# A sparse-attention and MLP kernel: another order and named PSUM banks for batch 0, and batch 1's steps moved by a group

## The chip, the cores and the metric

The kernel runs on one core of a Trainium2 chip. A core has a matrix engine (TensorE, PE in the profile), VectorE (DVE), ScalarE (ACT), GpSimd (POOL) and SyncE (SP), which work side by side and wait for each other through semaphores. Matmuls write to PSUM, a memory of 8 banks of 128 partitions x 512 fp32; VectorE and ScalarE read it from there. DMA queues move data between HBM and on-chip SBUF; SyncE and GpSimd issue them here. The metric is the device time of the program in microseconds, lower is better.

## The reference

Eight batches of eight heads, 576 tokens each, head size 64. Heads 0 to 3 attend locally (a token sees itself and the 31 before it), heads 4 to 7 with a stride (a token sees the earlier tokens whose position is equal modulo 32). The result goes through an MLP with a squared ReLU.

```python
scores = scale * np.matmul(q, k.transpose(0, 1, 3, 2))
mask_local = (rel >= 0) & (rel < stride)                                  # heads 0-3
mask_strided = (rel >= 0) & (pos[None, :] % stride == pos[:, None] % stride)  # heads 4-7
attn = softmax(np.where(masks, scores, -1e9))
x = np.matmul(attn, v).transpose(0, 2, 1, 3).reshape(4608, 512)
out = np.square(np.maximum(x @ w_in, 0)) @ w_out      # 512 -> 2048 -> 512
```

Inputs and output are float32; the kernel computes in bf16 with fp32 accumulation.

## The kernel before

**Units and chunks.** Heads go in pairs: unit u = 4*batch + pair. Pairs 0 and 1 are local, 2 and 3 strided; so units 0 and 1 are batch 0's local pairs, 2 and 3 its strided ones. Each pair's attention output is a 128-row strip of `xt[pair]`, which holds x transposed, all 4608 tokens. The MLP runs in 9 chunks of 512 tokens. A chunk has 16 groups of `mm1` (four matmuls over the four `xt` strips, L662, then ReLU on ScalarE, L668, and the square on VectorE, L669) and 16 groups of `mm2` (four matmuls each, L684; after every fourth a copy, L688, and a store).

**Order by hand.** The scheduler is off: every engine runs its instructions in the order in which the program issues them. The start (L814 to L850) issues the first loads, constants and masks. Then `BATCH0` is a list of steps that make batch 0's attention, ending with the first three `mm1` groups, split by `xt` strip (`P0 P23 P1`, strips 0, then 2 and 3, then 1; `FIRST` is that order). Then come the numbered groups of the MLP, and `PLAN` says which attention steps of later batches are issued ahead of which group. Groups 0 to 2 are empty (they are the `P` steps), 3 to 15 are the rest of chunk 0's `mm1`, 16 to 31 its `mm2`, 32 onward chunk 1, which needs batch 1.

**Steps** (unit or batch in the name, then the engine: a = ScalarE, v = VectorE, g = GpSimd):
- `c0q`: cast of q of local unit 0 to bf16 (L298). `T0q`: six TensorE transposes (L453) and a copy from PSUM (L460).
- `W0q0`, `W0q1`: the same for the strided heads of batch 0, in two tiles (L332, L337).
- `S0`: scores of unit 0 in two halves, each with two rows (heads): in batch 0 a matmul adds the mask as a bias (L482), then the scores (L493) and an exp per row and half (L503).
- `N2`: strided row sums by a matmul with ones (L583), reciprocal as Ln (L585) and Exp(-x) (L586). `O2`: strided values times weights (L607) and the multiply by the reciprocal into `xt` (L609).
- `D0.0`, `D0.1`: local values in two parts (L622), reciprocal (L627), multiply (L628). `E0`: transposes (L644) and the copy into `xt` (L647).
- `w2`: two matmuls on zeros into bank `py` (L719). `m`: memsets of zero blocks (L812). `H`: a shifted copy of v (L411).
- For batch 1: `l` loads q or k of the local pairs, `r` the strided rows, `U` and `V` the values, `o` a quarter of w_out (L429), `B` and `k` spread strided v and k (L398, L366), `s1.0` to `s1.2` strided scores (L538), `x1.0` to `x1.2` their sums, reciprocals and multiplies into `xt` (L549 to L568).

**PSUM.** Eight banks, each a tile of its own: two `ph`, one `py`, five `pt`. `bank("pt")` hands out the next in turn; in batch 0 the turn goes over the five `pt` and the two `ph`. A step that gets a bank waits until its last reader is done.

**Queues.** `load_qk_hw(0)` loads unit 0's q and k in fp32 through SyncE's queue; everything else until L850 goes through GpSimd's: strided q and k of batch 0, unit 1's q and k (L291), values, and w_in.

Of the kernel before, what the change touches and what calls it, by code (L numbers as in the profile page):

```python
# [12 lines left out]

FIRST = (0, 2, 3, 1)
NP = 3
BATCH0 = """
    c0qv c0ka T0qa c1kg w2 T0kv w2 S0 mk1v c1qv W0k0a w3 W0q0v W0k1a W0q1v T1qv w2 T1kv S2 S1 H0v D0.0 D0.1 S3
    D1.0 N3 D1.1 N2 E0a O3 O2 E1a w1 P0 P23 P1  # L20
"""
PLAN = """
0: l1q4+5 l1k4+5 z
1: r1q U1 mv1g
3: o0
4: r1k V1 mk0v
5: o1 l2k8+9 mbg
6: o2 o3 V2 mv0v
7: c4qv
8: c5qv  # L30
9: c4kv
10: l2q8+9 c5ka T4qa
11: T4kv T5qa
12: W1q0v T5ka
13: S4
14: W1q1v
16: W1k0a S5! B10v
17: W1k1a
18: D4.0 k10v mrg C2q C2k
19: k11v  # L40
20: D4.1 s1.0 B11v
21: D5.0 s1.1 U2
22: l3k12+13 s1.2
23: D5.1
24: E5v x1.0
26: X2k l3q12+13
27: E4v x1.1 c9kv
28: V3
29: x1.2 c8qv
30: c8ka c9qv  # L50
31: X2q
34: C3q B20v
35: T8kv B21v
37: T9kv
# [109 lines left out]
def kernel(  # L164
# [44 lines left out]
    banks = {nm: [psum.tile([128, 512], FP32, name=f"{nm}{i}") for i in range(n)]  # L209
             for nm, n in (("ph", 2), ("py", 1), ("pt", 5))}  # L210

    banks["b0"] = banks["pt"] + banks["ph"]
    in_b0 = [True]

    def bank(nm):
        if in_b0[0] and nm == "pt":
            nm = "b0"
        t = banks[nm].pop(0)
        banks[nm].append(t)
        while id(t) in unread:  # L220
            run_due(lambda x: x[1] == unread[id(t)])
        return t

    unread = {}

# [240 lines left out]
    def step_S(u, mode=0):  # L466
# [7 lines left out]
        s["e"] = e  # L474
        pss = [[None, None], [None, None]]
        for half in range(2):
            for row in range(2):
                pss[row][half] = bank("pt")
                if u < 4:
                    bias = bias_l[:, half].rearrange("p t c -> p (t c)") if local \  # L480
                        else bias_s.rearrange("p t c -> p (t c)")
                    nc.tensor.matmul(pss[row][half][0:kn, 0:S // 2], ident[0:kn, 0:kn], bias,  # L482
                                     start=True, stop=False, skip_group_check=True)
            for i in range(hn):
                t = half * hn + i
                klo = w * t
                for row in range(2):
                    rows = slice(64 * row, 64 * row + 64)
                    if not local:
                        lhsT, rhs = (a[rows, t // 4, t % 4, :] for a in (kT, qT))  # L490
                    else:
                        lhsT, rhs = kT[rows, klo:klo + kn], qT[rows, w * t:w * (t + 1)]
                    nc.tensor.matmul(pss[row][half][0:kn, w * i:w * (i + 1)], lhsT, rhs,  # L493
                                     start=u > 3, stop=True, skip_group_check=u < 4)

        for row in range(2):
            for half in range(2):
# [13 lines left out]
        if u < 4:  # L511
            for half in range(2):
                for row in range(2):
                    expo(row, half)
            return
        if mode == 1:
            for row in range(2):
                for half in range(2):
# [57 lines left out]
    def step_N(u):  # L576
        e, hw = st[u]["e"], S // 2
        kn = 128 if is_local(u) else SP_
        for half in range(2):
            pn = bank("pt")  # L580
# [4 lines left out]
            nc.scalar.activation(rv0[:, u, hw * half:hw * (half + 1)], pn[:, 0:hw], AF.Ln)  # L585
        nc.scalar.activation(rv0[:, u], rv0[:, u], AF.Exp, scale=-1.0)  # L586

    def step_O(u):
        s = st.pop(u)
        e, hw = s["e"], S // 2  # L590
        for half in range(2):
            po = bank("pt")
            rv = rv0[:, u, hw * half:hw * (half + 1)]
            if is_local(u):
                for t in range(NL // 2):
                    for h in range(2):
                        c = S * h + hw * half + QL * t
                        nc.tensor.matmul(po[64 * h:64 * h + 64, QL * t:QL * (t + 1)],
                                         vls[u][:, h, NL // 2 * half + t, 0:D], e[:, c:c + QL],
                                         start=True, stop=True)  # L600
                nc.vector.tensor_tensor(xt[u][:, hw * half:hw * (half + 1)], po[:, 0:hw], rv, op=ALU.mult)
                continue
            w = SP_
# [5 lines left out]
            nc.vector.tensor_tensor(  # L609
                xt[u][:, 0:S].rearrange("c (p j r) -> c p j r", j=NJ // 2, r=2)[:, :, :, half],  # L610
                po[:, 0:hw].rearrange("c (j p) -> c p j", p=SP_),
                rv.rearrange("c (j p) -> c p j", p=SP_), op=ALU.mult)
# [108 lines left out]
    idle = xt[0][:, T - 512:T]  # L721

    def first_part(kks):
        in_b0[0] = False
        for ff in range(NP):
            mm1(0, ff, kks, FIRST, None if ff < 2 else "py")

    def run_step(word):
        op, arg = word[0], word[1:]
        if op == "w":  # L730
            warm(int(arg))
# [72 lines left out]
    def memset_later(which, eng):  # L804
# [5 lines left out]
        else:  # L810
            t = (kbds if which[0] == "k" else vbds)[int(which[1])]
            eng.memset(t.rearrange("p n c -> p (n c)").bitcast(FP32), 0.0)  # L812
# [112 lines left out]
```

## Time and profile before

| | us |
|---|---|
| three timed runs | 304.89, 305.20, 307.47 |
| median | 305.2 |
| the profiled execution, in all | 304.5 |
| its span, first to last instruction | 302.8 |
| from the span's start to the first MLP matmul (L662) | 19.9 |
| matmuls of all 9 chunks, L662 and L684 on the chain that ended last | 38% and 37% of the span |

The profile is of one execution. TensorE's granted clock was 1.00 throughout. DMA engines are 97% busy in the first 10 us of the span and near that or above in the next 70. A timeline row gives the start, the duration, the engine, the line, what is written from what, the shapes, the number of instructions merged into the row, and in brackets the idle time of that engine before it and what ended it. A row of the list of waits says which engine and line waited for which, the total, how often, and the longest.

### The profile page before, as it was taken

How to read it: one execution, taken by the hardware profiler on the slowest of the kernel's cores; microseconds unless marked ns; L12 is line 12 of the kernel's file. 1: busy time of each engine (PE TensorE's matmuls, PEld its weight loads, DVE VectorE, ACT ScalarE, POOL GpSimd, SP SyncE). 2: the span in 40 equal slices, each digit the busy share in tenths (PEclk: the TensorE clock that was granted, in tenths of full speed). 3: DMA queues.
4: the chain of work that ended last, by engine and by line, in shares of the span. 5: the costliest groups of instructions: out<-in, count | busy, mean ns of one | idle time of the engine just before them, and what ended most of it. 6: DMA issues, size and time to landing. Idle time of an engine off the chain costs nothing.

```text
span 302.8 us, 5715 instructions
## 1 busy us (share of the span) xinstructions
PE 292.9 (97%) x2143; PEld 146.3 (48%) x2181; DVE 179.5 (59%) x465; ACT 173.2 (57%) x342; POOL 71.3 (24%) x105
## 2 busy tenths in 40 slices
PE   8988999999999999999999999999999999999996
PEld 3543555445555544454454445444454444444444
DVE  5668686888578686585558494676486524104400
ACT  3677853777657744773387446744775447216611
POOL 8734834007213018064300830000000000000000
PEclk9999999999999999999999999999999999999999
DMA  7999999997999999999998999511110110010011
GB/s 149 189 207 196 188 201 187 143 206 124 149 183 159 143 183 151 150 161 119 184 173 153 141 190 153 118 38 67 54 23 19 73 69 0 35 71 35 0 71 70
DMA packets 93643, 37.28 MB, mean 123 GB/s; under 512 B 78956, under 2 KB 87750, under 8 KB 93616
## 3 DMA queue, kind: packets, MB, share of 16 engines
q0 software_dynamic: 54960, 18.82, 62.8%
q1 hardware_dynamic: 38512, 18.03, 30.5%
q8 instruction: 17, 0.28, 0.4%
q14 instruction: 10, 0.08, 0.1%
q10 hardware_dynamic: 144, 0.07, 0.1%
HBM read 38.21 MB, written 9.44 MB: 157 GB/s over the span
## 4 chain that ended last, share of the span: by engine, by line
PE 89%; DVE 3%; issue 2%; DMA 2%; ACT 2%; POOL 0%; DVEq 0%; ACTq 0%; POOLq 0%
PE ph L662 38%; PE ph L684 37%; PE pt L493 2%; DMA w_out_b<-in_k_dram 2%; PE pt L622 2%; PE pt L538 1%; PE pt L552 1%; PE ph L709 1%; PE pt L453 1%; PE pt L549 1%; PE py L684 1%; DVE g_sb L669 1%; DVE xt L562 1%; PE pt L684 1%; ACT r L668 1%
## 5 line engine op out<-in xcount | busy, mean ns | idle before, releaser
L662 PE MATMUL ph<-xt,w_in_b 128*128 128x512 bf16 x548 | 130.5, 379 | 2.3 <-ACT xt L647 1.0
L684 PE MATMUL ph<-w_out_b,g_sb 128*128 128x512 bf16 x513 | 119.7, 379 | 0.8
L668 ACT ACTIVATE r<-ph 128x512 bf16<-128x512 f32 x142 | 84.8, 599 | 35.3 <-PE ph L662 30.2
L669 DVE TENSOR_TENSOR g_sb<-r 128x512 bf16<-128x512 bf16 x144 | 60.4, 422 | 63.8 <-ACT r L668 63.0
L662 PEld LDWEIGHTS <-w_in_b 128*128 128x128 bf16 x576 | 53.0, 97 | 59.7 <-issue 2.3
L684 PEld LDWEIGHTS <-g_sb 128*128 128x128 bf16 x560 | 51.7, 97 | 57.4 <-DVE g_sb L669 0.5
L688 ACT COPY y<-ph 128x512 f32<-128x512 f32 x33 | 19.4, 589 | 53.0 <-PE ph L684 53.0
L562 DVE TENSOR_TENSOR xt<-pt,rv 64x144 bf16<-64x144 f32 x84 | 34.0, 404 | 18.4 <-ACT rv L555 17.3
L503 ACT ACTIVATE e<-pt 128x288 bf16<-128x288 f32 (+1 forms) x68 | 24.0, 417 | 7.7 <-PE pt L493 7.7
L554 ACT ACTIVATE rv<-pt 128x432 f32<-128x432 f32 (+1 forms) x21 | 10.5, 501 | 13.8 <-PE pt L549 13.8
L628 DVE TENSOR_TENSOR x_l<-pt,rinv 96x384 bf16<-96x384 f32 x30 | 16.6, 554 | 1.0
L568 DVE TENSOR_TENSOR xt<-pt,rv 64x270 bf16<-64x270 f32 (+1 forms) x28 | 10.9, 432 | 8.5 <-ACT rv L555 8.4
L509 DVE TENSOR_TENSOR e<-e,mask_all 128x576 bf16<-128x576 bf16 x28 | 12.4, 453 | 3.9 <-ACT e L503 3.6
L539 ACT ACTIVATE e<-pt 128x432 bf16<-128x432 f32 (+1 forms) x21 | 10.4, 497 | 6.6 <-PE pt L538 6.6
L350 POOL DMA_DIRECT2D q_t<-in_q_dram x6 | 3.6, 602 | 44.0 <-DMA qT_s<-q_t 44.0
L419 POOL DMA_DIRECT2D vl<-in_v_dram x7 | 10.1, 1437 | 12.2 <-PE ph L684 6.9
L279 POOL DMA_DIRECT2D k_l<-in_k_dram x16 | 11.9, 751 | 2.9 <-PE pt L552 2.9
L279 POOL DMA_DIRECT2D q_l<-in_q_dram x16 | 11.8, 740 | 2.8 <-DMA k_l<-in_k_dram 1.4
L622 PEld LDWEIGHTS <-e 128*128 128x128 bf16 x192 | 9.1, 97 | 5.8 <-issue 0.4
L555 ACT ACTIVATE rv<-rv 128x432 f32<-128x432 f32 (+1 forms) x21 | 11.2, 533 | 0.7
L622 PE MATMUL pt<-vl,e 128*128 128x65 bf16 x180 | 9.9, 193 | 0.0
L350 POOL DMA_DIRECT2D k_t<-in_k_dram x6 | 3.2, 538 | 25.2 <-DMA kT_s<-k_t 25.2
(130 smaller groups left out, 216.8 us busy)
## 6 DMA issues: line engine op xcount, KB each, us to landing
out_dram<-y SPq DMA_DIRECT2D x35, 256.0 KB, 3.9
vl<-in_v_dram POOLq DMA_DIRECT2D x7, 384.0 KB, 12.4
w_in_b<-in_moe_w_in_dram POOLq DMA_DIRECT2D x4, 512.0 KB, 13.1
w_out_b<-in_moe_w_out_dram POOLq DMA_DIRECT2D x4, 512.0 KB, 13.1
q_t<-in_q_dram POOLq DMA_DIRECT2D x7, 288.0 KB, 6.6
k_t<-in_k_dram POOLq DMA_DIRECT2D x7, 288.0 KB, 5.8
v_st<-in_v_dram POOLq DMA_DIRECT2D x7, 216.0 KB, 8.5
k_l<-in_k_dram POOLq DMA_DIRECT2D x16, 72.0 KB, 7.9
```

The lines of the kernel that those rows point to most:

```text
L279: nc.gpsimd.dma_start(out=t[:, :, hh, :], in_=src[b, 2 * p + hh].rearrange("(t p) d -> p t d", p=QL))
L503: nc.scalar.activation(e[0:kn, lo:lo + S // 2], pss[row][half][0:kn, 0:S // 2], AF.Exp, scale=scale)
L509: nc.vector.tensor_tensor(x, x, m, op=ALU.mult)
L555: nc.scalar.activation(rv, rv, AF.Exp, scale=-1.0)
L562: nc.vector.tensor_tensor(to[:, :, NJ * part:NJ * (part + 1), par], of, by, op=ALU.mult)
L622: nc.tensor.matmul(po[:, n, :], e[:, c:c + 128], rhs[:, NL * part + n, 0:D + 1], start=True, stop=True)
L628: nc.vector.tensor_tensor(x, po[0:QL, :, 0:D], rinv[0:QL].to_broadcast([QL, NL, D]), op=ALU.mult)
L662: nc.tensor.matmul(ph, w_in_b[:, kk, 128 * ff:128 * (ff + 1)], xt[kk][:, 512 * c:512 * (c + 1)], start=(kk == order[0]), stop=(kk == order ...
L668: nc.scalar.activation(r, ph, AF.Relu)
L669: later(1, lambda: nc.vector.tensor_tensor(g[:, ff, :], r, r, op=ALU.mult))
L684: nc.tensor.matmul(py, g[:, ff, 128 * j:128 * (j + 1)], w_out_b[:, ff, :], start=(ff == 0), stop=(ff == 15))
L688: nc.scalar.copy(y, py)
```

## The change

The batch-0 list is reordered: unit 1's casts, transposes and scores come directly behind unit 0's and ahead of the strided transposes and scores; the casts and copies are dealt out to other engines; the MLP's first part runs over strips 2, then 0, then 1 and 3. Unit 1's q and k come through SyncE's queue in fp32, as unit 0's do, instead of GpSimd's.

All eight banks are now one tile `psb`. In batch 0 each step names its banks after a slash, and where it works on two banks, the number is the first of two neighbours: `S2/0,2` puts the first half into banks 0 and 1, the second into 2 and 3; `S0/0,1` puts the first into 0 and 1, the second into 1 and 2. The exps of a half, the Ln of `N`, the multiply of `O` and the reciprocal and multiply of `D` (new function `step_D0`, both parts at once) are one instruction over two banks.

In the plan, most steps of batch 1 move to the next group; the first quarter of w_out is loaded ahead of strided q; the memset of one block goes from VectorE in batch 0 to GpSimd; the E copies of batch 1 go to ScalarE; x1.1 and x1.2 come a group earlier.

```diff
-FIRST = (0, 2, 3, 1)
+FIRST = (2, 0, 1, 3)
 BATCH0 = """
-    c0qv c0ka T0qa c1kg w2 T0kv w2 S0 mk1v c1qv W0k0a w3 W0q0v W0k1a W0q1v T1qv w2 T1kv S2 S1 H0v D0.0 D0.1 S3
-    D1.0 N3 D1.1 N2 E0a O3 O2 E1a w1 P0 P23 P1
+    c0qa c0kv T0qa/6 w1/7 T0kv/4 w1/7 S0/0,1 c1qv c1kv T1qv/5 T1ka/6 w2/7 S1/0,1 W0q0v/4 W0q1v/5 w3/7 W0k0a/4
+    W0k1v/5 w1/7 S2/0,2 H0v S3/4,0 D0/2 N2/6 D1/4 E0a/0 O2/2 N3/6 O3/4 E1a/1 w2/5 P2 P0 P13
 """
 PLAN = """
 0: l1q4+5 l1k4+5 z
-1: r1q U1 mv1g
-3: o0
-4: r1k V1 mk0v
-5: o1 l2k8+9 mbg
-6: o2 o3 V2 mv0v
-7: c4qv
-8: c5qv
-9: c4kv
-10: l2q8+9 c5ka T4qa
-11: T4kv T5qa
-12: W1q0v T5ka
-13: S4
-14: W1q1v
-16: W1k0a S5! B10v
-17: W1k1a
-18: D4.0 k10v mrg C2q C2k
-19: k11v
-20: D4.1 s1.0 B11v
-21: D5.0 s1.1 U2
-22: l3k12+13 s1.2
-23: D5.1
-24: E5v x1.0
-26: X2k l3q12+13
-27: E4v x1.1 c9kv
-28: V3
-29: x1.2 c8qv
-30: c8ka c9qv
-31: X2q
+1: o0 mv1g
+3: r1q mk0v
+4: r1k mk1g
+5: U1 V1 mbg mv0v
+6: o1 o2
+7: o3 l2k8+9 V2
+8: c4qv
+9: c5qv
+10: c4kv
+11: l2q8+9 c5ka T4qa
+12: T4kv T5qa
+13: T5ka
+14: W1q0v
+15: S4 W1q1v
+17: W1k0a S5! B10v
+18: W1k1a
+19: k10v mrg C2q C2k D4.0
+20: k11v D4.1
+21: s1.0 B11v D5.0
+22: s1.1 U2
+23: l3k12+13 s1.2 D5.1
+24: x1.0
+25: E4a
+26: x1.1 X2k l3q12+13
+27: E5a
+28: x1.2 V3
+29: c9kv
+30: c8qv
+31: c8ka c9qv X2q
...
+    psb = psum.tile([128, 8, 512], FP32, name="psb")
+    all_banks = [psb[:, i] for i in range(8)]
+    banks = {"ph": [all_banks[i] for i in (6, 2)], "py": [all_banks[7]],
+             "pt": [all_banks[i] for i in (3, 1, 0, 4, 5)]}
+    places = []
     def bank(nm):
-        if in_b0[0] and nm == "pt":
-            nm = "b0"
+        if places:
+            return all_banks[places.pop(0)]
...
+    def bank_pair():
+        i = places.pop(0)
+        return all_banks[i:i + 2], psb[:, i:i + 2]
...
         for half in range(2):
+            if u < 4:
+                (pss[0][half], pss[1][half]), both = bank_pair()
...
+            if u < 4:
+                hw = S // 2
+                nc.scalar.activation(e[0:kn, 0:2 * S].rearrange("p (r c) -> p r c", r=2)[:, :, hw * half:hw * (half + 1)],
+                                     both[0:kn, :, 0:hw], AF.Exp, scale=scale)
...
+    def step_D0(u):
...
+        pos, both = bank_pair()
+        for part, po in enumerate(pos):
+            for n in range(NL):
+                c = QL * (NL * part + n)
+                nc.tensor.matmul(po[:, (D + 1) * n:(D + 1) * (n + 1)], e[:, c:c + 128], rhs[:, NL * part + n, 0:D + 1],
+                                 start=True, stop=True)
...
+        nc.vector.reciprocal(r, po[:, :, :, D:D + 1])
+        nc.vector.tensor_tensor(s["x"].rearrange("p (t h) d -> p h t d", h=2), po[:, :, :, 0:D],
+                                r.to_broadcast([QL, 2, NL, D]), op=ALU.mult)
...
     load_qk_hw(0)
+    load_qk_hw(1)
     load_str_rows(0, "q")
...
-    load_qk_local_sw(0, (1,))
     load_v0()
```

More of the change, by code (lines that the diff above doesn't have):

```diff
@@ L208 @@
     psum = ctx.enter_context(tc.tile_pool(name="psum", bufs=1, space=PS))
[L209 to L213, printed above, removed]
+    psb = psum.tile([128, 8, 512], FP32, name="psb")
[3 more added lines that the diff above has]
+    places = []
     def bank(nm):
-        if in_b0[0] and nm == "pt":
-            nm = "b0"
+        if places:
+            return all_banks[places.pop(0)]
         t = banks[nm].pop(0)
@@ L269, in load_qk_hw @@
             c = n_s + 8 * S if name == "q" else n_s
+            c += 24 * D * (u if name == "k" else -u)
             t = b0[0:QL, c:c + 24 * D].bitcast(FP32).rearrange("p (h c) -> p h c", h=2)
@@ L476, in step_S @@
         for half in range(2):
+            if u < 4:
+                (pss[0][half], pss[1][half]), both = bank_pair()
             for row in range(2):
-                pss[row][half] = bank("pt")
+                if u > 3:
+                    pss[row][half] = bank("pt")
                 if u < 4:
@@ L494, in step_S @@
                                      start=u > 3, stop=True, skip_group_check=u < 4)
+            if u < 4:
+                hw = S // 2
+                nc.scalar.activation(e[0:kn, 0:2 * S].rearrange("p (r c) -> p r c", r=2)[:, :, hw * half:hw * (half + 1)],
+                                     both[0:kn, :, 0:hw], AF.Exp, scale=scale)
+        if u < 4:
+            return
         for row in range(2):
@@ L509, in masks @@
             nc.vector.tensor_tensor(x, x, m, op=ALU.mult)
[L511 to L515, printed above, removed]
         if mode == 1:
@@ L578, in step_N @@
         kn = 128 if is_local(u) else SP_
-        for half in range(2):
-            pn = bank("pt")
+        pns, both = bank_pair()
+        for half, pn in enumerate(pns):
             for h in range(2):
@@ L584, in step_N @@
                                  start=True, stop=True)
-            nc.scalar.activation(rv0[:, u, hw * half:hw * (half + 1)], pn[:, 0:hw], AF.Ln)
+        r = rv0[:, u].rearrange("p (t c) -> p t c", t=2)
+        nc.scalar.activation(r, both[:, :, 0:hw], AF.Ln)
         nc.scalar.activation(rv0[:, u], rv0[:, u], AF.Exp, scale=-1.0)
@@ L589, in step_O @@
         s = st.pop(u)
[L590 to L603, printed above, removed]
+        e, hw, w = s["e"], S // 2, SP_
+        pos, both = bank_pair()
+        for half, po in enumerate(pos):
             for t in range(hw // w):
@@ L608, in step_O @@
                                      start=True, stop=True)
[L609 to L612, printed above, removed]
+        nc.vector.tensor_tensor(
+            xt[u][:, 0:S].rearrange("c (p j r) -> c p j r", j=NJ // 2, r=2),
+            both[:, :, 0:hw].rearrange("c r (j p) -> c p j r", p=SP_),
+            rv0[:, u].rearrange("c (r j p) -> c p j r", r=2, p=SP_), op=ALU.mult)
+    def step_D0(u):
+        s = st[u]
+        e = s["e"]
+        rhs = s["v"].rearrange("p h t d -> p (h t) d")
+        pos, both = bank_pair()
+        for part, po in enumerate(pos):
[3 more added lines that the diff above has]
+                                 start=True, stop=True)
+        po = both[0:QL, :, 0:NL * (D + 1)].rearrange("p h (n d) -> p h n d", d=D + 1)
+        s["x"] = xl_pool.tile([QL, 2 * NL, D], BF16, name="x_l")
+        rinv = small.tile([128, 2 * NL, 1], FP32, name="rinv0")
+        r = rinv[0:QL].rearrange("p (h n) o -> p h n o", h=2)
+        nc.vector.reciprocal(r, po[:, :, :, D:D + 1])
+        nc.vector.tensor_tensor(s["x"].rearrange("p (t h) d -> p h t d", h=2), po[:, :, :, 0:D],
+                                r.to_broadcast([QL, 2, NL, D]), op=ALU.mult)
     def step_D(u, part):
@@ L723, in first_part @@
     def first_part(kks):
-        in_b0[0] = False
         for ff in range(NP):
@@ L728, in run_step @@
     def run_step(word):
+        word, _, at = word.partition("/")
+        places[:] = [int(x) for x in at.split(",") if x]
         op, arg = word[0], word[1:]
@@ L750, in run_step @@
         elif op == "D":
-            u, part = arg.split(".")
-            step_D(int(u), int(part))
+            if "." in arg:
+                u, part = arg.split(".")
+                step_D(int(u), int(part))
+            else:
+                step_D0(int(arg))
         elif op == "E":
```

## The prediction

> **What bounds the kernel now.** I read the busy times on the page first, then TensorE's list of waits, then the timeline of the first 50 us, where all of the change lies.
>
> ```profile
> PE 292.9 (97%) x2143; PEld 146.3 (48%) x2181; DVE 179.5 (59%) x465; ACT 173.2 (57%) x342; POOL 71.3 (24%) x105
> ```
>
> TensorE is busy 97% of the span, and about 216 ns is what one 128x512 matmul occupies (in the chain of waits 16 take 3.45 us). So 302.8 us can only shrink by about 10 us of idle time, and a change moves the end only where it changes TensorE's waits or what stands in front of its steady work. TensorE's waits in the whole run:
>
> ```profile
> PE pt L453 <- DVE q_l L298: 1.1, 1, 1.1
> PE ph L662 <- ACT xt L647: 1.0, 1, 1.0
> PE ph L332 <- DMA w_out_b<-in_k_dram: 0.6, 1, 0.6
> PE pt L493 <- ACT e L503: 0.5, 1, 0.5
> PE ph L662 <- DVE xt L568: 0.3, 1, 0.3
> ```
>
> The second and third lie in batch 0, the others in batch 1. No wait on w_out appears, so "w_out sooner" removes nothing. The end of batch 0 in the timeline (start, duration, engine and line):
>
> ```profile
> 15.17 1.33 ACT L503 ACTIVATE e<-pt 72x288 bf16<-72x288 f32 x4 [0.25 <-PE pt L493]
> 17.91 0.69 ACT L585 ACTIVATE g_sb<-pt 128x288 f32<-128x288 f32 x2
> 18.63 0.68 ACT L586 ACTIVATE g_sb<-g_sb 128x576 f32<-128x576 f32 x1
> 19.22 1.16 ACT L647 COPY xt<-pt 128x576 bf16<-128x576 bf16 x2
> 19.35 1.21 DVE L609 TENSOR_TENSOR xt<-pt,g_sb 128x288 bf16<-128x288 f32 x2
> 19.89 0.59 PE L662 MATMUL ph<-xt,w_in_b 128*128 128x512 bf16 x2 [1.04 <-ACT xt L647]
> ```
>
> The last exp ends at 16.50, then ScalarE runs two reciprocals (Ln, Exp) and the xt copies, and the first MLP matmul starts at 19.89. Its 12 matmuls (P0, P23, P1) then run without a gap: 19.89 + 12 x 0.216 = 22.5. **That 22.5 is the mark**: later, TensorE is nearly full.
>
> **Batch 0, part by part.** TensorE runs in program order, so a bank that is still being read holds everything behind it.
>
> *The second local pair's loads* leave GpSimd's queue (L291: 0.67 + 0.63 us of issue) for SyncE's, behind 0.41 and 0.43 us of issue. Landing of its k is not in the trace. Early bound: q0 landed at 0.82 + 3.5 = 4.3 and k0 at 1.29 + 3.9 = 5.2, 0.9 apart, so q1 6.1 and k1 7.0. Late bound: the total read is the same as before, and then k1 landed at 4.93 + 5.6 = 10.5. I take 8.5, between. The Trainium skill (DMA: Bandwidth & Descriptors, Queues, rings and completion order) says that a DMA engine takes packets in turn from the queues that have work; by that the local rows would share with the strided ones, and both sets would end near the late bound. The trace can't separate this: strided k took 6.2 us beside SyncE's loads, those took 3.9.
>
> *Pair 0's scores (S0, banks 0 and 1).* A named pair is the bank named and the next, so the first half uses banks 0 and 1 and the second 1 and 2. The second half's first matmul must wait until the exp over banks 0 and 1 has read. I price that exp at 0.66 us (288 columns take 0.41, a 576-column copy from PSUM 0.64, a 576-column ScalarE row 0.68), 0.6 in a queue; two single ones take 0.31 each in a queue, so the merging itself wins nothing. VectorE's cast is 0.49 against 0.83 on ScalarE, so kT is ready at 7.3 (before 7.51). Half 0's scores 7.3 to 7.75, exp to 8.45, half 1 8.5 to 9.2, exp to 9.9.
>
> *Pair 1 (S1, banks 0 and 1 again).* Behind S0 on TensorE: T1q 9.1, its copy (0.75) to 10.3; T1k, whose ScalarE copy (0.64) queues behind S0's exp, to 10.45. Half 0 10.5 to 10.9, exp to 11.6, half 1 11.7 to 12.3: the same wait a second time.
>
> *Strided transposes and scores.* W0q0 starts at 12.26 (before, the first strided transpose ran at 9.05 when its rows landed). Four tiles share banks 4 and 5, so W0k0 waits for W0q0's copy (0.48, to 13.2) and is itself copied at 13.9 to 14.55; S2's scores start at 14.7 against 12.04. But pair 1's exps are now behind, so after S2 and S3 (0.6 us a half, as the old rows have it) the last exp ends at 17.6 against 16.5: +1.1.
>
> *Tail.* D0 now multiplies both parts in one VectorE step: 0.25 + 0.95 (96x384 takes 0.55, of which about 0.4 grows with columns), to 18.65. E0a's transposes wait for it, and O2 and N3 are queued behind E0a on TensorE: N3 18.7 + 0.3 + 0.6 + 0.5 = 20.05. Ln 0.66, Exp 0.68: 21.5. O3's one multiply of 576 columns (L609: 0.61 each for two halves, so 1.15): 22.65. Before, the last multiply ended at 19.35 + 1.21 = 20.55.
>
> *The warm matmuls `w2/5`* write bank 5, and O3 used banks 4 and 5. So they wait for O3's multiply, and P2, P0 and P13, queued behind, wait too, though xt2 is ready at about 21.0 and xt0 at 19.8. Two warm matmuls (0.43) and all 12 MLP matmuls (2.6) then follow 22.7: 25.7. Without that wait P2 and P0 would have run before 22.7.
>
> The same walk with the same durations over the old order ends at 23.2 where the trace has 22.5, so it is 0.7 too long; I take that off: 25.0, **+2.5 us**. Of this, the shared bank 1 is worth about 1.1 and bank 5 about 1.8; without both the walk ends at 22.8, 0.4 before its own old mark of 23.2. Bounds: -0.7 (both covered, k1 early) to +3.4 (k1 at 9.6 adds 0.8).
>
> **Batch 1.** *The 1.1 us before T4q.* VectorE is late there, not the data (rows issued at 12.0 landed by 29.5):
>
> ```profile
> 25.90 1.23 DVE L812 MEMSET kb<- 128x1408 f32 x1 [0.24 <-issue]
> 27.98 1.23 DVE L812 MEMSET vb<- 128x1408 f32 x1 [0.24 <-issue]
> 29.41 0.34 DVE L298 COPY q_l<-xt 96x768 bf16<-96x768 bf16 x1
> 29.80 0.28 PEld L453 LDWEIGHTS <-q_l 96*128 96x128 bf16 x6 [1.54 <-DVE q_l L298]
> ```
>
> T4q moves a group (0.87 us) back, both memsets stay ahead of the cast and one more square (0.36) is in front. P13 ends ff 0 four matmuls before the end instead of two, so VectorE starts +2.5 - 0.43 = +2.1 later and casts at 29.41 + 2.1 + 0.36 = 31.9, ready 32.2; TensorE arrives at 25.0 + 8 x 0.866 = 31.9. Wait 0.3 instead of 1.1: **-0.7** (0 to -1.1). kb1's memset (1.23) goes from VectorE in batch 0 (it lay at 7.75 beside TensorE's work) to GpSimd, which idles for ring room there: nothing. GpSimd's new order puts 512 KB of w_out ahead of strided q, which landed at 31.0; that piece took 2.1 us after the one before it (34.2 against 32.1), so q lands at about 33, before W1q0 needs it at 35: nothing.
>
> *S5.*
>
> ```profile
> 37.85 0.41 ACT L503 ACTIVATE e<-pt 128x288 bf16<-128x288 f32 x1
> 38.15 0.65 ACT L326 COPY kT_s<-pt 128x576 bf16<-128x576 bf16 x1
> 38.31 0.30 PE L493 MATMUL pt<-qT,kTl 64*128 64x96 bf16 x6 [0.49 <-ACT e L503]
> ```
>
> S5's second half waits for S4's fourth exp. S5 now follows S4 by two groups, not three, so that exp is issued behind W1k0's copy: from W1k0 on TensorE 0.47 to the copy, 0.64, 0.41, less 0.5 of TensorE work: wait 1.0 instead of 0.5, **+0.5** (-0.5, if the lighter ScalarE catches up, to +0.8).
>
> *The end of batch 1.* x1.2 comes a group earlier, both E copies (0.46 each) leave VectorE, and c9k (0.36) moves behind. VectorE is then done about 1 us before chunk 1 needs it: **-0.3** (0 to -0.4). ScalarE had 2.1 us idle before each reciprocal there, which covers two copies of 0.64; uncovered they'd cost 0.6.
>
> **Sum**: 2.5 - 0.7 + 0.5 - 0.3 = +2.0 us. Nothing later changes. The profiled run took 304.5 with a span of 302.8, so 306.5 by it; the median shown is 305.2, 0.7 above it, and gives **307.2**. By all lower ends: -0.7 - 1.1 - 0.5 - 0.4 = -2.7 (302.5); by all upper ones +4.2 (309.4).
>
> **Rivals.** *A, faster.* The tail is quicker than I count, so that O3's multiply is over when TensorE reaches `w2/5` after E1's transposes (point of decision: about 21.0 in my walk), and pair 1 fills the 0.6 us in which TensorE waited for strided k. Then batch 0 ends 0.4 earlier, TensorE at 22.1 + 6.9 = 29.0 meets a cast ready at about 29.3, and the total is -0.4 - 0.7 - 0.3 = -1.4: 303.8. For: one multiply instead of two, fewer waits. Against: the two-reciprocal chain alone (0.66 + 0.68 + 1.15) is longer than E1's 0.4.
> *B, clearly slower.* Pair 1 lands near the late bound: every step after T1q is 0.8 to 1.6 later, and as batch 0 has nothing else to do, that reaches the mark: +2.8 to +3.6, about 308.4. It decides from k1 landing after about 8.5. For: DMA engines are 97% busy in the first 10 us. By the skill's turn-taking it would be this.
> *C, nothing.* VectorE's and ScalarE's savings in batch 1 are larger and pay the wait back: 305.2.
>
> **How the numbers follow.** Forecast 0.60 (its own range 306.1 to 308.2), A 0.20, B 0.12, C 0.08. The range 303.5 to 308.9 takes in A's middle and most of B, and leaves out about 0.15. This kernel's measurement can tell about 1%, 3.05 us. Faster by more than that (below 302.2) lies past A's sum: 0.03. Slower by more (above 308.2): two thirds of B and the forecast's upper tail, 0.16. Within: 0.81.
>
> **What would show it.** TensorE waiting for ScalarE's e between S0's halves and S1's; L719's last warm matmuls starting just after the last xt multiply, with the first MLP matmul behind them near 23; first MLP part over near 25; T4q's wait about 0.3; S5's about 1.0; no wait on xt before chunk 1. If the warm matmuls run before that multiply, A holds; if a cast of pair 1 waits for its DMA past 9, B.

## The result and the profile after

The changed kernel took 312.89 us (median of four runs, 311.43 to 317.5), against 305.2 before (304.89 to 307.47): a ratio of 1.0241 [1.0208, 1.0274], which leaves out the slowest execution (317.5, at a granted clock of 0.962). It is 2.4% slower, and outside the predicted range (303.5 to 308.9). Its profiled execution took 311.43 us with a span of 309.7, so 6.9 us more than before's 304.5 and 302.8. All times below are from profiled executions and counted from the span's start, unless they are called medians.

The page of the kernel after, the busy times and the granted clock in 40 slices:

```profile
PE 298.3 (96%) x2181; PEld 148.5 (48%) x2181; DVE 179.4 (58%) x457; ACT 174.9 (56%) x334; POOL 70.1 (23%) x103
...
PEclk9689999999999999999999999999999999999999
```

TensorE is busy 5.4 us longer (298.3 against 292.9). Of this, 3.5 lie in batch 0, up to the end of the first MLP part (22.9 against 19.4); the rest is spread over the later stages, where before's trace lacks records (2143 matmuls against 2181, at the same 2181 weight loads), and is no loss. In batch 0 the second and third slices, 7.7 to 23 us, show a granted clock below full speed. Before's profiled execution had 1.00 throughout. So there are two kinds of loss to look for, waits and slower matmuls. TensorE's waits, as the list of waits of the kernel after has them (line numbers of this kernel: L460 is a local transpose, L492 a mask, L503 a score, L738 the matmuls on zeros):

```profile
PE psb L738 <- DVE xt L610: 1.7, 1, 1.7
PE psb L460 <- DVE k_l L305: 1.6, 2, 1.0
PE psb L492 <- ACT e L507: 1.5, 2, 0.7
```

Batch 0 in the timeline, the rows on the path to the first MLP matmul (start, duration, engine, line, in brackets the wait ahead of it):

```profile
8.70 0.93 DVE L305 CAST q_l<-g_sb 96x768 bf16<-96x768 f32 x1 [0.80 <-DMA g_sb<-in_q_dram]
9.00 0.40 PE L492 MATMUL psb<-w_out_b,ident 128*128 128x288 bf16 x2 [0.74 <-ACT e L507]
...
10.47 0.56 DVE L305 CAST k_l<-g_sb 96x768 bf16<-96x768 f32 x1 [0.85 <-DMA g_sb<-in_k_dram]
...
11.08 0.66 PE L460 MATMUL psb<-ident,k_l 96*128 96x96 bf16 x6 [0.97 <-DVE k_l L305]
...
18.52 0.34 PE L503 MATMUL psb<-qT_s,kT_s 64*72 64x72 bf16 x8
...
25.08 1.13 DVE L610 TENSOR_TENSOR xt<-psb,g_sb 128x576 bf16<-128x576 f32 x1 [0.34 <-ACT g_sb L598]
...
26.26 0.59 PE L738 MATMUL psb<-xt 128*128 128x512 bf16 x2 [1.74 <-DVE xt L610]
...
26.69 3.62 PE L681 MATMUL psb<-xt,w_in_b 128*128 128x512 bf16 x16
```

Unit 1's k was predicted to land at 8.5; its cast waits for it until 10.47. The six transposes behind it take 0.66 us where six took 0.43 before: the clock has halved. The strided scores start at 18.52 (before 12.04, predicted 14.7). From there the tail is as predicted: the last multiply of O3 ends at 26.21, and the zero matmuls in bank 5 start right behind it. The first MLP matmul runs at 26.69 instead of 19.89, and the first MLP part is over near 29.3 instead of 22.5: +6.8. From that mark to the end it is 280.4 us, and it was 280.3. **All of the loss lies in batch 0; batch 1's plan as a whole is worth nothing here.**

The clock, from the windows of the kernel after (for each stretch its length, then busy us and instructions of PE, PEld, DVE, ACT and POOL, then the granted clock, the DMA share and GB/s):

```profile
8.00:9.00 1.00, 0.26 (x6) 0.21 (x7) 0.30 (x1) 0.65 (x1) 1.00 (x2) 1.00 1.18 208
9.00:10.00 1.00, 0.96 (x14) 0.54 (x13) 0.62 (x1) 0.32 (x1) 0.35 (x2) 1.00 1.60 194
10.00:11.00 1.00, 0.11 (x3) 0.00 (x0) 0.53 (x2) 0.33 (x1) 0.58 (x1) 0.80 2.14 167
11.00:12.00 1.00, 0.92 (x8) 0.65 (x9) 0.69 (x2) 0.22 (x1) 0.32 (x1) 0.50 1.95 172
...
17.00:18.00 1.00, 1.00 (x15) 0.73 (x14) 0.00 (x0) 0.17 (x1) 0.00 (x0) 0.79 1.25 208
18.00:19.00 1.00, 0.99 (x15) 0.48 (x11) 0.88 (x2) 0.57 (x2) 0.99 (x2) 1.00 1.23 205
```

TensorE works 0.26 and 0.11 us of two of the three microseconds in which it waits for unit 1; then the clock is half from about 10.6 to 17.4.

The loads (the last figure is the time from issue to landing). Before, those issued from 1 to 4 us:

```profile
g_sb<-in_q_dram SPq DMA_DIRECT2D x1, 288.0 KB, 3.5
g_sb<-in_k_dram SPq DMA_DIRECT2D x1, 288.0 KB, 3.9
w_out_b<-in_q_dram POOLq DMA_DIRECT2D x1, 288.0 KB, 6.0
w_out_b<-in_k_dram POOLq DMA_DIRECT2D x1, 288.0 KB, 6.2
```

After, those of the window from 2.2 to 4 us:

```profile
w_out_b<-in_q_dram POOLq DMA_DIRECT2D x1, 288.0 KB, 8.2
g_sb<-in_q_dram SPq DMA_DIRECT2D x1, 288.0 KB, 6.9
g_sb<-in_k_dram SPq DMA_DIRECT2D x1, 288.0 KB, 8.2
w_out_b<-in_k_dram POOLq DMA_DIRECT2D x1, 288.0 KB, 8.6
```

The g_sb rows are local pairs (unit 0 before, unit 1 after), the w_out_b rows the strided ones, which use that block as a stage. Strided q and k take 2.2 and 2.4 us longer. And unit 1's k, issued at 2.25, lands at 10.4, where before, by GpSimd's queue and issued 2.7 us later, it landed at 10.5: **the pair that the new order puts first does not come sooner, and the pair that it puts second comes later.**

### The profile page after: what moved, and what is told of

It reads as the page before. It is cut to its first block, busy times and chain, and to the rows that moved or that the text cites. A ratio compares the mean times of both kernels' runs of the same rounds, so it can differ in the third digit from the quotient of the medians.

```text
span 309.7 us, 5728 instructions
## 1 busy us (share of the span) xinstructions
PE 298.3 (96%) x2181; PEld 148.5 (48%) x2181; DVE 179.4 (58%) x457; ACT 174.9 (56%) x334; POOL 70.1 (23%) x103
## 3 DMA queue, kind: packets, MB, share of 16 engines
q1 hardware_dynamic: 38928, 18.62, 29.3%
## 4 chain that ended last, share of the span: by engine, by line
PE 89%; DVE 4%; DMA 3%; ACT 2%; issue 1%; SPq 0%; DVEq 0%
PE psb L703 38%; PE psb L681 38%; DMA g_sb<-in_k_dram 3%; PE psb L503 2%; PE psb L641 2%; PE psb L549 1%; PE psb L563 1%; PE psb L460 1%; PE psb L728 1%; PE psb L560 1%; PE psb L738 1%; DVE g_sb L688 1%; PE psb L492 1%; DVE xt L573 1%; ACT r L687 1%
## 5 line engine op out<-in xcount | busy, mean ns | idle before, releaser
L681 PE MATMUL psb<-xt,w_in_b 128*128 128x512 bf16 x576 | 132.9, 379 | 0.0
L703 PE MATMUL psb<-w_out_b,g_sb 128*128 128x512 bf16 x560 | 129.0, 379 | 0.0
L687 ACT ACTIVATE r<-psb 128x512 bf16<-128x512 f32 x144 | 85.9, 599 | 36.5 <-PE psb L681 32.8
L707 ACT COPY y<-psb 128x512 f32<-128x512 f32 x35 | 20.6, 590 | 52.9 <-PE psb L703 52.8
L573 DVE TENSOR_TENSOR xt<-psb,rv 64x144 bf16<-64x144 f32 x84 | 34.0, 405 | 18.6 <-ACT rv L566 17.5
L519 ACT ACTIVATE e<-psb 128x288 bf16<-128x288 f32 x56 | 19.9, 416 | 6.3 <-PE psb L503 6.3
L565 ACT ACTIVATE rv<-psb 128x432 f32<-128x432 f32 (+1 forms) x21 | 10.5, 501 | 11.1 <-PE psb L560 11.1
L647 DVE TENSOR_TENSOR x_l<-psb,rinv 96x384 bf16<-96x384 f32 x28 | 15.5, 554 | 1.0
L579 DVE TENSOR_TENSOR xt<-psb,rv 64x270 bf16<-64x270 f32 (+1 forms) x28 | 11.0, 432 | 8.5 <-ACT rv L566 8.3
L550 ACT ACTIVATE e<-psb 128x432 bf16<-128x432 f32 (+1 forms) x21 | 10.4, 496 | 6.5 <-PE psb L549 6.5
L738 PE MATMUL psb<-xt 128*128 128x512 bf16 x20 | 9.1, 588 | 3.0 <-DVE xt L610 1.7
```

The lines of the kernel that those rows point to most:

```text
L519: nc.scalar.activation(e[0:kn, lo:lo + S // 2], pss[row][half][0:kn, 0:S // 2], AF.Exp, scale=scale)
L573: nc.vector.tensor_tensor(to[:, :, NJ * part:NJ * (part + 1), par], of, by, op=ALU.mult)
L647: nc.vector.tensor_tensor(x, po[0:QL, :, 0:D], rinv[0:QL].to_broadcast([QL, NL, D]), op=ALU.mult)
L681: nc.tensor.matmul(ph, w_in_b[:, kk, 128 * ff:128 * (ff + 1)], xt[kk][:, 512 * c:512 * (c + 1)], start=(kk == order[0]), stop=(kk == order ...
L687: nc.scalar.activation(r, ph, AF.Relu)
L703: nc.tensor.matmul(py, g[:, ff, 128 * j:128 * (j + 1)], w_out_b[:, ff, :], start=(ff == 0), stop=(ff == 15))
```

## The experiments

My theory after this reading: three things add up, late data (about 1.7 us), the halved clock (about 2.2) and the two shared banks of the prediction. Rivals: the banks alone explain it; the queue alone explains it; the plan costs something that batch 0 hides. Zero matmuls (`w`) write values that nobody reads, so adding or removing them leaves the result as it is. The results together (ratios to the kernel before, run on the same chip; the clock is the mean of the profiled execution, and other executions of the same kernel can differ):

| kernel | median us | ratio | first MLP matmul at | clock |
|---|---|---|---|---|
| before | 305.2 | | 19.89 | 1.000 |
| after | 312.89 | 1.0241 [1.0208, 1.0274] | 26.69 | 0.989 |
| after, bank 5 free | 309.56 | 1.0128 [1.0055, 1.0202] | 25.82 | 0.989 |
| after, bank 1 not shared | 311.94 | 1.0196 [1.0121, 1.027] | 25.64 | 0.987 |
| after, gaps filled | 311.81 | 1.0163 [1.0063, 1.0263] | 24.86 | 0.988 |
| after, unit 1 by GpSimd's queue | 311.62 | 1.0195 [1.0117, 1.0273] | 27.10 | 0.989 |
| before, unit 1 by SyncE's queue | 309.99 | 1.017 [1.014, 1.0201] | 22.58 | 1.000 |
| before, new plan | 305.77 | 1.0014 [0.9985, 1.0044] | 20.94 | 1.000 |
| after, both banks | 308.1 | 1.0105 [1.0073, 1.0136] | 24.60 | 0.988 |
| the same, gaps filled | 306.68 | 1.0046 [1.0025, 1.0068] | 22.38 | 1.000 |
| the same, strided loads later | 306.3 | 1.0032 [1.0003, 1.006] | 21.62 | 1.000 |
| the same, less filling | 304.41 | 0.998 [0.9961, 0.9999] | 20.23 | 1.000 |
| strided first again | 305.97 | 1.0027 [0.9998, 1.0057] | 19.33 | 1.000 |
| the same, strided q of batch 1 sooner | 305.2 | 0.9979 [0.9941, 1.0017] | 19.43 | 1.000 |
| strided first, old plan | 304.67 | 0.9999 [0.9975, 1.0023] | 19.37 | 1.000 |

### One part of the change undone

**Bank 5.** The zero matmuls ahead of the MLP go to bank 0, which is free by then.

```diff
-    ... E0a/0 O2/2 N3/6 O3/4 E1a/1 w2/5 P2 P0 P13
+    ... E0a/0 O2/2 N3/6 O3/4 E1a/1 w2/0 P2 P0 P13
```

> The two warm matmuls ahead of the MLP write bank 0 instead of bank 5; nothing else differs from the changed kernel. If the wait for O3's multiply is worth what the prediction said, TensorE's wait of 1.7 us before L738 is gone, P2 starts when xt2 is written (24.75 in the changed kernel's trace), P0 behind it at 25.4, P13 when xt1 and xt3 are there (25.6 and 26.2), and the first MLP part is over at about 27.4 instead of 29.3: -1.9 us, and the total falls by 1.5 to 1.9. Rival, the wait is covered because P13 needs O3's product anyway: no more than -0.5.

The median is 3.3 us lower than after's, the span 1.5. The wait of 1.74 is gone; the list of this kernel's waits shows what is left of it, at the first strip that really needs O3:

```profile
PE psb L681 <- DVE xt L610: 0.2, 1, 0.2
```

The MLP starts only 0.9 sooner because in this execution T1k ran still later (11.85 against 11.08), and the half clock lasted until 19.4. The gate of bank 5 is a cost as large as it was priced, but it is about one quarter of the loss.

**Bank 1.** S0 and S1 take four banks instead of three.

```diff
-    ... S0/0,1 ... S1/0,1 ...
+    ... S0/0,2 ... S1/0,2 ...
```

> S0 and S1 use banks 0 to 3 (0,2) instead of 0 to 2 (0,1), so the two waits of TensorE for an exp (0.74 us each) go. By the prediction's walk both lie on the path: -1.1 us or more. By the trace of the changed kernel only the second can: behind S0's second half TensorE waits for the casts of unit 1, whose data land at 8.7 and 10.4 whatever S0 does. Then -0.7, a little more if the clock is still half there. Either way T1k's transposes stay at about 11.1.

Both waits of 0.74 on the exp are gone from the list, and the first MLP matmul runs 1.05 sooner, although unit 1's k was later in this execution (T1k at 11.85). But the span is 1.2 longer than after's: the clock was half from 12.6 to 16.0 and again from 26.3 to 29.7, behind the 1.7 us in front of bank 5, and that second time it slowed the MLP itself. With the interval the median can't be told from after's. In this execution, curing one wait alone moved part of the slow clock to another place.

**The clock.** Zero matmuls fill TensorE's waits while unit 1 comes: three between the halves of S0 and of S1, four ahead of T1k.

```diff
-    ... T1qv/5 T1ka/6 ...
+    ... T1qv/5 w4/7 T1ka/6 ...
...
+                if u < 2 and half == 0:
+                    places.insert(0, 7)
+                    warm(3)
```

> Matmuls on zeros are put where TensorE stands idle: three between the halves of S0 and of S1 and four ahead of T1k's transposes. They add no wait. Theory: the granted clock halved from 10.6 to 17.4 us because TensorE was too idle before; kept busy it stays at 1.00, the stretch from T1k's transposes to S2's scores shrinks from 7.4 to about 5.2 us, and the total falls by about 2. Rival, the stretch is bound by the copies and casts between the transposes: clock 1.00 but no more than -0.5. If the fill doesn't hold the clock, +0.5 or nothing.

Nothing that is computed got shorter, but the strided scores start at 16.30 instead of 18.52. From T1k's transposes to these scores it is 5.10 us (11.20 to 16.30, with three more zero matmuls in it) against 7.44 in after (11.08 to 18.52): the half clock costs about 2.3 us there. The total did not follow. Windows of this kernel:

```profile
8.00:12.00 4.00, 3.01 (x28) 1.44 (x28) 2.01 (x3) 1.27 (x3) 2.08 (x4) 1.00 1.72 182
...
20.00:24.00 4.00, 1.87 (x48) 1.46 (x49) 3.62 (x5) 3.21 (x6) 1.21 (x3) 0.79 1.26 205
24.00:28.00 4.00, 3.73 (x9) 1.43 (x10) 0.00 (x0) 0.00 (x0) 1.82 (x3) 0.50 1.27 204
```

The clock now falls in the tail, at 22.3, where TensorE waits for bank 5, and the first MLP matmuls run at half speed. One of the four executions kept the full clock and took 307.88; the others (0.995, 0.988, 0.987) 311.6 to 312.65. So the clock's share in that stretch is shown, and a fall in front of the MLP costs as much as the one it replaced.

**The queue.** Unit 1's loads go back to GpSimd's queue; the new order stays.

```diff
-    load_qk_hw(1)
...
+    load_qk_local_sw(0, (1,))
```

> Unit 1's q and k go through GpSimd's queue again, behind strided q and k, in bf16. Theory: the DMA engines are full until about 10.5 us, so unit 1's k lands near 10.4 by either queue; T1k's transposes stay within 0.3 us of 11.1, the strided rows land 2 us sooner and nobody waits for them: -0.3 to +0.3 in the total (GpSimd's issues cost its later loads 1.3 us, which are not waited for). Rival, SyncE's queue as such is slow here because it shares with GpSimd's: T1k 1 us or more earlier.

T1k starts at 11.40 against 11.08: unit 1's k (it landed near 10.7) comes equally late by either queue, and by the intervals the time can't be told from after's. With local scores first, a late k is the same loss whoever issues it.

### One part alone on the kernel before

**The loads alone.** Unit 1 by SyncE's queue, with before's order, banks and plan (its stage shifted so that both pairs fit).

```diff
+            c += 24 * D * (u if name == "k" else -u)
...
+    load_qk_hw(1)
     load_str_rows(0, "q")
...
-    load_qk_local_sw(0, (1,))
```

> The kernel before with unit 1's q and k loaded through SyncE's queue, order and banks as before. Theory: the engines are full, so what SyncE's queue takes early the strided rows get later: strided k lands near 11.6 instead of 9.0, and as batch 0 works on it first there, the first MLP matmul moves from 19.9 to 21.5 or later: total +1.5 to +2.5. Rival, the loads only change queues and nothing is late: within 0.3.

This part alone is 1.7% slower (three of its four executions had a clock below 1.00, the profiled one not). The list of waits of this kernel has it at the top, on the strided transposes:

```profile
PE ph L333 <- DMA w_out_b<-in_k_dram: 2.5, 1, 2.5
```

Before, that wait was 0.6 and the transposes ran at 9.05; here at 11.76. Unit 1's k was cast at 10.71, against 10.56 before. So the moved loads take 2.7 us from the strided rows and give unit 1 nothing. The first MLP matmul is 2.7 later, but the span 4.2 longer. Of the other 1.5 us, TensorE's waits show 0.3 more before T4q (1.35 against 1.05), 0.16 before T4k, and 0.46 at 94.2 us for a VectorE multiply (L510) that before does not have; about 0.6 stays unplaced.

**The plan alone.** Before's batch 0 with the new plan (and one memset moved with it from VectorE to GpSimd).

```diff
-    ... w2 S0 mk1v c1qv W0k0a ...
+    ... w2 S0 c1qv W0k0a ...
 PLAN = """ (as in the change)
```

> The kernel before with the new plan for batch 1 and nothing else (kb1's memset is on GpSimd in the plan). The prediction gave the plan -0.5 us (T4q's wait -0.7, S5's +0.5, the end of batch 1 -0.3). The changed kernel's trace says nothing is gained: from the end of the first MLP part to the end it takes 280.4 us (309.7 - 29.3), the kernel before 280.3 (302.8 - 22.5). So 0 by the trace, -0.5 by the prediction; and no loss of over 1 us, or the plan is part of the cause.

It makes no difference that can be measured: the T4q wait is 0.5 instead of 1.1, and batch 0 ends 1.05 later instead. The cause of that is odd. Its timeline around the shifted copy of v (L412):

```profile
12.76 0.75 POOL L430 DMA_DIRECT2D w_out_b<-in_moe_w_out_dram  x1
12.88 2.25 DVE L412 COPY vl<-vl 32x1280 bf16<-32x1280 bf16 x1
...
13.50 1.29 POOL L813 MEMSET vb<- 128x1408 f32 x1
...
15.18 0.31 PE L623 MATMUL ph<-vl,e 128*128 128x65 bf16 x5 [0.84 <-DVE vl L412]
```

The copy took 0.48 before. Here it lasts until 0.34 us after GpSimd's memset has ended, and TensorE waits 0.84 for it.

### The theory as a whole

**Both banks.** Both bank edits together, nothing else.

```diff
-    ... S0/0,1 c1qv c1kv T1qv/5 T1ka/6 w2/7 S1/0,1 ... E1a/1 w2/5 P2 P0 P13
+    ... S0/0,2 c1qv c1kv T1qv/5 T1ka/6 w2/7 S1/0,2 ... E1a/1 w2/0 P2 P0 P13
```

> As the kernel with all three cures, without its added matmuls on zeros (none behind S0 and none ahead of T1k, two at the end as in the changed kernel). Theory: the clock is a cause of its own; TensorE stands idle for unit 1's rows from about 8 to 11 us and the granted clock halves behind it in most executions: 1.5 to 4 us slower than with the fill (308 to 310.5), with clocks below 1.00 in the list of runs. Rival, the half clock came from the bank waits: then clocks stay at 1.00 and it is within 0.7 us of 306.7.

The expectation refers to the kernel that follows here, which ran first (306.7). This one is 1.4 us slower, with a clock below 1.00 each time, as expected.

**Both banks and the gaps filled.** As before, with nine zero matmuls more where TensorE waits for unit 1, and two more ahead of the MLP.

```diff
-    ... S0/0,2 c1qv c1kv T1qv/5 T1ka/6 w2/7 S1/0,2 ... E1a/1 w2/0 P2 P0 P13
+    ... S0/0,2 w3/7 c1qv c1kv T1qv/5 w6/7 T1ka/6 w2/7 S1/0,2 ... E1a/1 w4/0 P2 P0 P13
```

> The changed kernel with separate banks for the halves of S0 and S1, bank 0 for the last warm matmuls, and matmuls on zeros in the idle stretches (three behind S0, four more ahead of T1k, two more at the end). Theory: bank waits and clock add up. No half clock anywhere, first MLP part over at 24.0 to 25.0 instead of 29.3, total 4 to 5 us below the changed kernel, 305.5 to 307 on the scale where before is 304.8, so still not faster than before: the late local pair remains. Rival, the clock falls in another stretch as it did when only one wait was filled: then 2 us or less is won.

The list has six zero matmuls ahead of T1k, where the expectation says four. The time, 306.68, is as expected.

The pair is the cleanest evidence for the clock as a cause of its own. Without filling all four executions had 0.988 to 0.994; with it all seven had 0.999 or more, and the intervals, each against the kernel before on the same chip, don't meet. Windows of the kernel without filling:

```profile
8.00:9.00 1.00, 0.60 (x10) 0.22 (x8) 0.00 (x0) 0.94 (x2) 1.00 (x2) 1.00 1.18 212
9.00:10.00 1.00, 0.00 (x0) 0.00 (x0) 0.54 (x1) 0.30 (x1) 0.22 (x1) 0.94 1.84 178
10.00:11.00 1.00, 0.66 (x6) 0.45 (x6) 0.01 (x1) 0.00 (x0) 0.12 (x1) 0.50 2.03 150
11.00:12.00 1.00, 0.02 (x1) 0.03 (x2) 0.70 (x2) 0.00 (x0) 0.57 (x1) 0.50 1.74 180
```

And with filling:

```profile
9.00:10.00 1.00, 0.36 (x6) 0.36 (x8) 0.57 (x1) 0.00 (x0) 0.21 (x1) 1.00 1.60 184
10.00:11.00 1.00, 0.94 (x7) 0.40 (x5) 0.23 (x1) 0.00 (x0) 0.68 (x1) 1.00 2.24 164
11.00:12.00 1.00, 0.98 (x10) 0.47 (x9) 0.99 (x2) 0.15 (x1) 0.00 (x0) 1.00 1.94 177
```

Both leave the data late. With the banks and the clock cured, about 1.5 us of the 7.7 remain; by the theory they are the late data.

**The data too.** The last kernel, with the strided rows issued by GpSimd behind its masks (at 3.2 and 4.0 us instead of 1.4 and 2.8).

```diff
-    load_str_rows(0, "q")
...
-    load_str_rows(0, "k")
...
+    load_str_rows(0, "q")
+    load_str_rows(0, "k")
```

> As the kernel with all three cures (separate banks, bank 0 for the last warm matmuls, fill), but GpSimd issues strided q and k behind its masks (from about 2.9 us on) instead of at 1.4 and 2.8, so that SyncE's loads of unit 1 have the engines to themselves for longer. Theory: what decides is how many bytes are in flight ahead of a row, by whichever queue. Then unit 1's k lands at 7.5 to 8.5 instead of 10.5, T1k's transposes move from 11.4 to 8.5 to 9.0, the strided rows land by 11.5, the first MLP part is over 1.0 to 2.5 us earlier (25.0 there) and the total falls by as much, to about 305. Rival: the loads through SyncE are slow of themselves, or the strided rows then become the bound; no more than 0.5 is won.

A miss in size: 0.4 us of the median, 0.8 at the first MLP matmul. That is the size that the rival gave, but not for its reason, as the data did come: unit 1's k, issued at 2.25 as in the changed kernel, landed at 7.75.

```profile
g_sb<-in_k_dram SPq DMA_DIRECT2D x1, 288.0 KB, 5.5
```

But T1k ran only at 10.64, because the zero matmuls put there against the gap were now in its way. So the filling was cut to one matmul in each place:

```diff
-    ... S0/0,2 w3/7 c1qv c1kv T1qv/5 w6/7 T1ka/6 ...
+    ... S0/0,2 w1/7 c1qv c1kv T1qv/5 w1/7 T1ka/6 ...
```

> As the kernel with deferred strided loads, with one fill matmul behind S0 and one ahead of T1k instead of three and six. Unit 1's k lands at 7.8, so T1k's transposes can start near 9.0 instead of 10.6 and S1 follows near 10.5; the strided rows land at 8.8 and 10.4, so they are not late. Theory: the first MLP part is over at 22.5 to 23.0 instead of 24.2 and the total is 304.5 to 305.3, level with before: local first, with its data really first, costs nothing and wins nothing. Rival: with less fill the clock halves again, 307 or more.

Its timeline, the cast of unit 1's k and its transposes:

```profile
7.92 0.74 DVE L305 CAST k_l<-g_sb 96x768 bf16<-96x768 f32 x1
...
9.12 0.42 PE L460 MATMUL psb<-ident,k_l 96*128 96x96 bf16 x6
```

Of the waits for unit 1 only 0.2 us is left (on its q), the clock is 0.998 or more in all ten executions, and they lie between 304.27 and 304.76. That is 0.2% below the kernel before: the new order is as good as the old one once its data really come first. Whether it is also steadier ten executions can't tell, as the kernel before keeps its clock in about six of seven. It is the fastest kernel here by median, though the gain is at the edge of what can be told.

### The old order with the new instructions

Strided first again, unit 1 by GpSimd's queue, but the two-bank instructions and the new plan kept, with banks chosen so that none is shared:

```diff
-    c0qa c0kv T0qa/6 w1/7 T0kv/4 w1/7 S0/0,1 c1qv c1kv T1qv/5 T1ka/6 w2/7 S1/0,1 W0q0v/4 W0q1v/5 w3/7 W0k0a/4
-    W0k1v/5 w1/7 S2/0,2 H0v S3/4,0 D0/2 N2/6 D1/4 E0a/0 O2/2 N3/6 O3/4 E1a/1 w2/5 P2 P0 P13
+    c0qa c0kv T0qa/6 w1/7 c1kg T0kv/4 w2/7 S0/0,2 c1qv W0k0a/4 w3/7 W0q0v/5 W0k1a/6 W0q1v/0 T1qv/1 w2/7 T1kv/5
+    S2/2,6 S1/0,4 H0v D0/2 N2/6 S3/0,4 D1/2 E0a/0 O2/6 N3/4 O3/0 E1a/3 w2/5 P2 P0 P13
```

> The strided steps come ahead of unit 1's again and unit 1's loads are on GpSimd's queue, as before; kept are the two-bank instructions and the plan, with banks chosen so that no half waits for the other and N2 ahead of S3. Theory: the order against the landing times is the main loss, so this is level with before or better: first strided transposes near 9.1, first MLP part over at 21.5 to 22.5, clock 1.00, total -1.0 to 0 against before. Rival, the two-bank instructions themselves cost (an exp waits for both rows of a half): +1 or more against before.

The first MLP matmul runs at 19.33, 0.56 sooner than before, but the time is level with before (four of the ten executions had 0.988 to 0.994), and in the profiled one the gain is lost in batch 1. The list of waits of this kernel shows a wait that none of the others above has:

```profile
PE psb L329 <- DMA q_t<-in_q_dram: 2.2, 1, 2.2
```

The new plan loads strided q of batch 1 behind a quarter of w_out. In the changed kernel TensorE comes late enough not to see it. Two ways to cure it: strided q ahead of that quarter again, or the old plan altogether.

```diff
-1: o0 mv1g
-3: r1q mk0v
-4: r1k mk1g
-5: U1 V1 mbg mv0v
+1: r1q U1
+3: o0 mk0v mv1g
+4: r1k mk1g V1
+5: mbg mv0v
```

> The kernel with strided first, two-bank instructions and free banks, in whose trace only one new wait is left: 2.2 us of TensorE for strided q of batch 1, which the plan loads behind the first quarter of w_out. Here strided q comes ahead of that quarter again, and GpSimd's memset behind it. Theory: the wait goes and the batch-0 gain is kept: first MLP part over at about 22.0, -2 us against the kernel with that wait, -1 to -2 against before (303 to 304). Rival: VectorE's casts are late there instead (T4q's wait of about 1 us comes back) and it is level with before.

With the old plan instead:

> The same batch 0 with the whole plan of before (only kb1's memset on GpSimd in it). Theory: as the kernel beside it, but T4q comes a group earlier and waits about 0.6 to 1.0 us for VectorE's cast, and the last multiply of batch 1 is waited for again (0.3): 0.3 to 1.0 us slower than its neighbour, 0.5 to 1 us faster than before. Rival: the plan of after has no worth at all beside its load order; then the two are equal.

In both the wait for q is gone, and both are level with the kernel before; the 1 to 2 us and 0.5 to 1 us that were expected did not come. In the one with the old plan TensorE waits 1.4 us ahead of T4q, in place of 1.1: the half microsecond won in batch 0 is partly waited off there. (Its profiled execution took 306.21 us, 1.5 above its median, and shows a wait of 1.7 us on a transfer into `xt` too, so its rows are not typical.) These kernels differ from before also in bank choice and in the order of some steps, so the two-bank instructions are not alone on trial; together with those they neither win nor lose anything that can be measured.

## Why the prediction was wrong

It said slower, and by the right mechanisms, but 2.0 us of 6.9. Step by step:

- **Landing of unit 1's k: the step that failed first.** I took 8.5, the middle of 7.0 and 10.5; it landed at 10.4, the late bound. The early bound came from unit 0's loads, the first in line. The late bound, "the total read is the same", was the better argument. My upper bound for batch 0 did not use it: it put k1 at 9.6 (+0.8), and 10.5 would have added 1.7. (The 97% do not show by themselves that the engines are full, as that share goes above 1, to 2.14 between 10 and 11 us; the moved loads show it.) T1k ran at 11.08, which is 1.7 later than my walk had it. The Trainium skill (DMA: Bandwidth & Descriptors, Queues, rings and completion order) has the engines take turns between queues; by that both sets end near the late bound, and they did: unit 1's k at 10.4, strided k at 11.4 instead of 9.0. Rival B, given 0.12, was what happened to the data, and by the prediction's own sign (a cast of pair 1 that waits for its DMA past 9). Its 308.4 was still too low, because it had no clock in it.
- **The clock: a term that was left out.** I priced waits as idle time alone. Behind these waits TensorE's clock also halved for 6.8 us, which cost about 2.3 us on the path. The profile of before, at 1.00 throughout, didn't show this; what it did show is that the old list spends ten matmuls on zeros at its gaps, and I asked only what they cost.
- **The 0.7 taken off** for a walk that was too long over the old order: whether the new path had that slack can't be told from the sum below.
- **Bank 1: the waits right, the price too high.** Two waits of 0.74 on the exp, as described. But behind the first one TensorE waits 0.97 for unit 1's k anyway, so by the trace only the second counts, not the 1.1 of the walk.
- **Bank 5: right.** 1.74 predicted as 1.8, the zero matmuls starting 0.05 us after O3's multiply; undoing it took 1.5 from the span.
- **The tail: right.** From the last exp to the end of O3's multiply 4.8 us, predicted 5.0.
- **Batch 1: right in kind, off in sizes that cancel.** T4q's wait is gone (predicted 0.3 of 1.1), but T4k waits 0.63 for its cast, which stands on VectorE behind a cast of c5q that took 0.95 instead of 0.35 (see the last section). S5 waits 0.73 in two parts (predicted 1.0, before 0.49). No x is waited for before chunk 1, but a transpose of E waits 0.28. From the end of the first MLP part on the sum is +0.1 (280.4 against 280.3), where I had -0.5; the plan alone on the kernel before is worth nothing either. "w_out sooner" is worth nothing, as predicted, and costs 2.2 us where batch 0 ends early enough to see strided q late.

The sum, with what was measured: 2.5 as predicted, 1.7 for the data and 2.3 for the clock give 6.5, or 7.2 without the 0.7 taken off, against 6.8 at the end of the first MLP part. The 2.3 is from two executions of different kernels, and the terms overlap, so this is a rough account. The undoing of the parts supports it in another order: the two banks together take the median from 312.89 to 308.1, the filling to 306.68, the strided loads behind unit 1's and less filling to 304.41.

Open are about 0.6 us of the kernel with the loads alone, and what exactly makes the clock fall.

## What to carry to other kernels

In the first 10 us of this kernel a load came sooner only when other loads were issued later: moving it to another queue gave its own row nothing and cost the others over 2 us, and issuing the others at 3.2 and 4.0 us brought it 2.7 us forward. Price a gap on TensorE twice, as idle time and as a possible fall of the clock, and look for where that fall goes when a gap is cured. A bank named for filler matmuls is a gate for everything queued behind them, so give fillers a bank whose last reader is long done.

## What the runs showed of the hardware

**The clock falls in pieces.** In the profiled executions it is 1.00 or 0.50, and a fall lasts 6.8 us (after 10.6 to 17.4, bank 5 free 12.6 to 19.4, gaps filled 22.3 to 29.1, unit 1 by GpSimd's queue 11.1 to 17.9, both banks 9.9 to 16.7) or half of that (bank 1 not shared, 12.6 to 16.0 and 26.3 to 29.7). If other executions fall to half as well, their half-speed time is span x (1 - clock) x 2: 6.8 us in after's two executions at 0.989, about 14 in the one at 0.978 (313.64 us) and 24 in the one at 0.962 (317.5). A single long wait does not decide it: the kernel with the loads alone waited 2.5 us in one piece at full clock in its profiled execution, while after's fell half a microsecond into a wait of 0.97 (the longest ahead of it was 0.74), with 2.0 us of work between 7 and 11 us. Other executions of the kernel with the loads alone had 0.989 to 0.994. Even the kernel before falls at times: 10 of the 71 executions that ran beside the experiments had 0.988 to 0.994 and took 306.7 to 309.0 us. The change made a rare fall a regular one (all four executions of after). The Trainium skill (TensorE: Matmul & The Clock Gate, What's actually happening) describes a free-running window of about 3.4 us over which activity is judged; by it falls would last whole windows and vary from run to run. The 6.8 us (two such windows), the 3.4 and the spread agree with that, but its section Why this matters for your kernels asks for an idle gap of over about 3 us, and here shorter ones sufficed.

**A VectorE copy can wait for GpSimd.** In the kernel after the shifted copy of v took 1.61 us instead of 0.48, and again it ends 0.34 us after GpSimd's memset. Both rows from its timeline:

```profile
18.55 1.29 POOL L835 MEMSET kb<- 128x1408 f32 x1
18.57 1.61 DVE L418 COPY vl<-vl 32x1280 bf16<-32x1280 bf16 x1
```

In the plan kernel it began during a DMA issue of GpSimd's, and outlasted that and the memset behind it. The cast of c5q took 0.95 instead of 0.35 beside a DMA issue of 1.50. The Trainium skill (SBUF — State Buffer, Who interferes with whom) says that the two engines share a port pair, for some of VectorE's instructions, copies among them, as an exclusive lock, so that the one that comes second stands still until the other is done; the 0.34 us after the memset's end agrees. It stands within 0.01 in three more kernels in which the two overlap (bank 5 free, 1.82 us; both banks and the gaps filled, 0.57; the last of the local-first kernels, 2.20). My prediction put GpSimd's new order at nothing. In after TensorE was late enough that the slow copy cost nothing; in the plan kernel it cost 0.84 us. The slow cast of c5q is argued, not tested, to be behind T4k's wait of 0.63 in after: in the plan kernel that cast took 0.34, and T4k does not wait.
